# Absent rows read row 0 instead of needing cleared buffers, and Pool drains its finished transfers twice before the end

## The chip, the cores and the metric

The kernel runs on one core of a Trainium2 chip. The metric is the time of one execution on the device in microseconds (us), the median over several runs. Lower is better. A core has five engines that run side by side and wait for one another through semaphores: TensorE (PE, matrix products; PEld is its loading of weights), VectorE (DVE), ScalarE (ACT), GpSimd (Pool) and SyncE (SP, which here only issues transfers). Sixteen DMA engines move data between the main memory (DRAM) and the core's memory (SBUF). SP and ACT issue transfers through hardware queues. Pool issues its own through a software queue[...].

## What is computed

Two layers, one after the other.

```python
# attention with decay, in blocks of 64 positions: q, k, v are (4, 8, 768, 64)
intra = (qb @ kb.T * Dmask) @ vb
inter = (qb * lam_pow) @ kv_state
out[:, :, sl] = intra + inter
kv_state = lam_block * kv_state + (kb * rev_pow).T @ vb
...
# mixture of experts on the 3072 rows of 512 numbers that this gives
logits = xn @ en.T / tau          # x and the 8 expert embeddings, normalized
expert_idx = argmax(logits)       # one expert for each row
gate_w = softmax(logits)[expert_idx]
for e in range(8):
    h = maximum(x[mask] @ w1[e], 0)          # w1[e] is 512 x 1024
    out[mask] = gate_w[mask] * (h @ w2[e])   # w2[e] is 1024 x 512
```

Each row of the result belongs to one expert, so the second layer needs its rows sorted by expert.

## The kernel before

The work is ordered by hand (`tc.manual_schedule()`); every engine executes its instructions in the order in which the code writes them.

**The attention loop** (L774) runs over 24 tiles of 128 rows, `i` = 0 to 23. In each, PE transposes q and k (`pe_Tq`, `pe_Tk`), forms the scores (`pe_ST`, L383), multiplies them with v (`pe_O`) and updates the state (`pe_kv`). The finished tile is transposed back (`pe_X`) into `xg`, and `write_x` (L461) writes a group of tiles to the row store `x_dram`, one row of 272 words for each token: 512 numbers of 16 bits, then the gate's weight. A second set of steps routes the rows of a group as soon as it is complete: `pe_z`, `pe_sel`, `rt_a` to `rt_d`, `rt_n` (the norm, on Pool, L512) and `make_list`. These steps are hung on iterations by `at(i, slot, ...)`. The loop runs slot "pool" and then slot "w" at the end of an iteration. Groups have four tiles at first; the last two, 5 and 6 (GL), have two.

**The slots of the experts.** There are ten slots `r`. Experts 0 and 1 are split: slots 0 and 1 take their rows among the first 16 tiles, so that they can begin while attention still runs, and slots 2 and 3 take the rest. Slots 4 to 9 are experts 2 to 7. A slot has full tiles of 128 rows (2, 1 or 3 of them) and half a tile of 64 rows. The half tiles of two neighbouring slots share one tile, named `("h", r)`. That makes 24 full tiles and 5 shared ones, 29 in all, or 3712 places for 3072 rows. The rest stay empty.

**Row numbers.** The lists are built by matrix products of comparisons (`pe_list`) and added up in `lacc`. `decode` turns a list entry into a row number. An empty place comes out as LB = 4096, which is no row. `ids(r0, r1)` decodes the slots r0 to r1 - 1 into `lid` and puts the numbers of the shared tiles into `lh`.

**Gather and scatter.** `gather(r, g)` (L643) reads the 128 rows of tile g of slot r from `x_dram` into `x_e`. It is an indirect transfer with a bounds check: a place whose number is past the end is skipped, so its part of the buffer keeps what it held. For this reason `gather(r, None)` allocates the buffer and clears it with a Pool memset (L649) ahead of time: three buffers before the loop (L732), and twelve in the tail between attention and experts (L963 to L968). `put` (L900) multiplies a finished tile by the gate's weights on DVE and scatters the 128 rows to the output with an indirect transfer on Pool (L904), where empty places are skipped too. It then issues the gathers that the table `after` names for that place. There are 29 scatters; `n_scat[0]` counts them.

**Weights.** The weights of experts 0 to 2 are cast to 16 bits by their transfer, which the Pool queue issues: twelve transfers in the order expert 0 w1 (two halves), w2 (two halves), expert 1, expert 2. `load_w` issues the next one in slot "w" of the iterations 7, 9, 11, 13, 15, 16, 17, 18, 19, 20, 21 and 22. Those of experts 3 to 7 come later through SP in forty parts (`part_load`) and DVE casts them (`part_cast`).

**Early use.** Slots 0 and 1 are gathered in slot "pool" of iterations 19 (two tiles of slot 0), 20 (the shared tile and tile 0 of slot 1) and 21 (tile 1 of slot 1). PE transposes them in iterations 21, 22 and 23 (`early_xT`, L666).

**The tail and the experts** (from L961). The routing of the last group runs here: the norm on Pool (L512), `rt_c` on DVE (L562 is its first instruction) with the exponential on ACT (L568), the list, `ids(ES, NR)`, and the gathers of slots 2 and 3 and of their shared tile. Between these steps PE computes the first layer of slot 0 (`pe_L1`, L826, with ReLUs on ACT, L828). Then PE alternates first layers, second layers (`pe_L2`, L925, and `pe_L2h`, L934) and transposes of the next slot (`pe_xT`, `pe_xTh`) to the end.

**The close.** A branch (L1034) skips a part for slots that overflow. After it the program's last instructions (L1133) wait for all engines and drain them. Pool's queue has issued 12 weight loads, 29 gathers and 29 scatters by then.

Of the kernel before, what the change touches and what calls it, by code (L numbers as in the profile page):

```python
# [13 lines left out]
I32 = mybir.dt.int32  # L14
AF = mybir.ActivationFunctionType
ALU = mybir.AluOpType
# [4 lines left out]
def kernel(  # L21
# [12 lines left out]
    nc = tc.nc  # L34
    P = 128
# [19 lines left out]
    ES = 2  # L55
    TA = 16
    NR = ES + E
    HT = P // 2
    FULL = [2] * ES + [1] * ES + [3] * (E - ES)
# [4 lines left out]
    VR, GR = 32 * P, 4  # L64
    NL = NR * GR


    LB = 4096
# [15 lines left out]
    const = ctx.enter_context(tc.tile_pool(name="const", bufs=1))  # L84
# [12 lines left out]
    n_out = sum(FULL) + NR // 2  # L97
# [107 lines left out]
    lrow = const.tile([P, P], FP32, name="lrow")  # L205
    lacc = const.tile([P, NL], FP32, name="lacc")
    ltmp = const.tile([P, NL], FP32, name="ltmp")
    lid = const.tile([P, NL], I32, name="lid")
    lh = const.tile([P, NR // 2], I32, name="lh")
    nsq_all = const.tile([P, R], FP32, name="nsq_all")  # L210
    ohcum = [const.tile([P, E], FP16, name=f"ohcum{n}") for n in range(2)]
    en_n = const.tile([E, DC, 2, D], FP32, name="en_n")
# [233 lines left out]
    def pe_X(t):  # L446
        gi, j = group_of[t]
        if j == 0:
            xg[gi] = xgp.tile([P, 4, XW], I32, name="xg", tag="xg")
            nc.gpsimd.memset(xg[gi][:, :, DW:], 0)  # L450
        xv = xps.rearrange("p (u a d) -> p a u d", u=2, a=DC)
        for a in range(DC):
            nc.tensor.transpose(xv[:, a], xT_of(t, a), ident)  # L453
        sq = xtp.tile([P, DM], FP16, name="sq", tag="sq", bufs=1)
        nc.scalar.activation(sq, xps, AF.Square, accum_out=nsq_all[:, t : t + 1])  # L455
        nc.scalar.copy(xg[gi][:, j, 0:DW].bitcast(FP16), xps)
# [21 lines left out]
    def pe_sel(t):  # L478
        for s in range(2):
            gi, j = group_of[t - 1 + s]  # L480
            nc.tensor.matmul(z_of(gi)[:, j, :], zT[t][:, ds(P * s, P)], sel,
                             start=True, stop=True, skip_group_check=True)
# [25 lines left out]
    def rt_n(gi):  # L508
        tl = groups[gi]
        nt = len(tl)  # L510
        rt.setdefault(gi, {})["nrm"] = rsm.tile([P, 4], FP32, name="nrm", tag="nrm")[:, 0:nt]
        nc.gpsimd.tensor_tensor(rt[gi]["nrm"], nsq_all[:, tl[0] : tl[0] + nt], half[:, 0:nt],  # L512
                                op=ALU.pow)
# [94 lines left out]
    idl, xe, xTe, hT = {}, {}, {}, {}  # L608
    moe_x, moe_t = [moe_x1], [moe_t1]

    def decode(io, acc, tmp):
        nc.vector.scalar_tensor_tensor(tmp, acc, -1.0, acc, op0=ALU.mult, op1=ALU.min)
        nc.vector.scalar_tensor_tensor(tmp, acc, 0.0, tmp, op0=ALU.is_lt, op1=ALU.add)
        nc.vector.tensor_scalar(io, tmp, float(LB), None, op0=ALU.add)


    def ids(r0, r1):
        cols = slice(GR * r0, GR * r1)
        decode(lid[:, cols], lacc[:, cols], ltmp[:, cols])
        lr = lid.rearrange("p (n s g) -> p n s g", s=2, g=GR)  # L620
        r = r0
        while r < r1:
            q = r
            while q < r1 and FULL[q] == FULL[r]:
                q += 1
            nc.vector.tensor_copy(lh[0:64, r // 2 : q // 2], lr[0:64, r // 2 : q // 2, 0, FULL[r]])
            r = q
        nc.vector.tensor_copy(lh[64:128, r0 // 2 : r1 // 2], lr[64:128, r0 // 2 : r1 // 2, 1, 0])
        for r in range(r0, r1):
            g0 = r % 2  # L630
            idl[r] = lid[:, GR * r + g0 : GR * r + g0 + FULL[r]]
            if r % 2 == 0:
                idl["h", r] = lh[:, r // 2 : r // 2 + 1]


    def col0(r):
# [6 lines left out]
    def gather(r, g):  # L643
        if r not in xe:
            n = 1 if isinstance(r, tuple) else FULL[r]
            n1 = 1 if moe_x[-1] is moe_x1 else ES + NR // 2 - 1
            xe[r] = moe_x[-1].tile([P, n, XW], I32, name="x_e", tag=f"x_e{n}",
                                   bufs={1: n1, 2: ES, 3: E - ES}[n])
            nc.gpsimd.memset(xe[r], 0)  # L649
        if g is None:  # L650
            return
        first = r in range(ES) or r == ("h", 0)
        nc.gpsimd.indirect_dma_start(  # L653
            out=xe[r][:, g, :], out_offset=None, in_=x_dram[0 : TA * P] if first else x_dram[:],
            in_offset=bass.IndirectOffsetOnAxis(ap=idl[r][:, g : g + 1], axis=0),
            bounds_check=N - 1, oob_is_err=False)

    def xt_tile(r):
# [27 lines left out]
    def at(i, slot, fn, *a):  # L686
        todo.setdefault((i, slot), []).append((fn, a))
# [5 lines left out]
    for gi in range(GL):  # L693
        n = groups[gi][-1] + 1
# [14 lines left out]
        if n + 3 < R - 1:  # L709
            at(n + 3, "rank", lambda zr, gi=gi: pe_list(gi, zr[:, 64:128]))  # L710
            at(n + 3, "z", ev_list, gi)
            if gi == 3:
                at(n + 3, "z", ids, 0, ES)
    for i in (7, 9, 11, 13, 15, 16, 17, 18, 19, 20, 21, 22):
        at(i, "w", load_w, 1)
    for i, r, g in ((19, 0, 0), (19, 0, 1), (20, ("h", 0), 0), (20, 1, 0), (21, 1, 1)):
        at(i, "pool", gather, r, g)
# [11 lines left out]

    pool_ks(0)  # L730
    pool_ks(1)
    for r in (0, 1, ("h", 0)):  # L732
        gather(r, None)
    pe_Tk(0)
    pe_Tq(0)
    decay0(1)
# [105 lines left out]
    n_scat = [0]  # L842

    with (
# [15 lines left out]
        h = "h"  # L860
# [39 lines left out]
        def put(y_ps, r, g):  # L900
            y = moe_y.tile([P, DM], FP32, name="y_sb", tag="y_sb")
            nc.vector.tensor_scalar(y, y_ps, xe[r][:, g, DW : DW + 1].bitcast(FP32), None,  # L902
                                    op0=ALU.mult)
            nc.gpsimd.indirect_dma_start(  # L904
                out=out_views[n_scat[0]],
                out_offset=bass.IndirectOffsetOnAxis(ap=idl[r][:, g : g + 1], axis=0),
                in_=y[:],
                in_offset=None,
                bounds_check=N - 1,
                oob_is_err=False,  # L910
            )
            for x in after.get(n_scat[0], []):
                if x == h:
                    gather(pairs.pop(0), 0)
                else:
                    gather(*x)
            if n_scat[0] > 1:
                part_cast()
            n_scat[0] += 1

        def pe_L2(r, g):
            w = w_tiles[(expert(r), 2)]
            y_ps = ps_y.tile([P, DM], FP32, name="y_ps", tag="y")
            for fc in range(FC):
                nc.tensor.matmul(y_ps, hT[r][:, fc, ds(col0(r) + P * g, P)], w[:, fc, :],  # L925
                                 start=(fc == 0), stop=(fc == FC - 1))
            put(y_ps, r, g)
# [32 lines left out]

        pe_z(R - 1, kaz[:, 0:256])  # L961
        pe_X(R - 1)
        for x in (ES, ES + 1, ("h", ES)):  # L963
            gather(x, None)
        rt_n(GL)
        for r in range(2 * ES, NR, 2):
            for x in (r, r + 1, ("h", r)):
                gather(x, None)  # L968
        pe_sel(R - 1)
        rt_a(GL)  # L970
        rt_a2(GL)
# [10 lines left out]
        for gi in range(GL - 2, GL + 1):  # L982
            pe_list(gi, kaz[:, 320:384], first=(gi == GL - 2), last=(gi == GL))
        ev_list(GL)
        ids(ES, NR)
        gather(2, 0)
        gather(3, 0)
# [46 lines left out]
    with tc.If(mreg > 0, preferred_fallthrough_block=True, label="past"):  # L1034
        with (
# [11 lines left out]
            with tc.For_i(0, NR) as r:  # L1047
# [14 lines left out]
                with tc.For_i(0, end):  # L1062
                    l_ps = of_ps.tile([P, 1], FP32, name="of_l", tag="of_l")
                    for t in range(R):
# [12 lines left out]
                        in_offset=bass.IndirectOffsetOnAxis(ap=io[:, 0:1], axis=0),  # L1077
# [15 lines left out]
                    for fc in range(FC):  # L1093
# [44 lines left out]
```

## Time and profile before

| | before |
|---|---|
| time, median of 3 runs | 274.88 us (272.67 to 275.95) |
| span of the profiled execution | 266.9 us |
| PE busy | 240.6 us (90%) |
| DVE, ACT, Pool busy | 143.6, 123.0, 145.8 us |
| memsets of `x_e` (L649) | 15, from 314 to 768 ns each |
| Pool's transfers | 12 weight loads, 29 gathers, 29 scatters |
| gather on Pool (L653), scatter on Pool (L904) | medians 1,038 and 1,074 ns |
| weight load on Pool (L320, L322) | medians 788 and 783 ns |

Busy time is that of an engine's own instructions. Issuing a transfer from SP, waiting, branching and draining are not counted. The profiled execution is one run; its span ends with the last barrier. Two rates of PE's clock occur, 1.0 and 0.5 of full speed, and the profile gives their mean over a stretch as the granted clock. A transfer has two times, that of its issue by an engine and that of its landing, which the semaphore records give.

### The profile page before, as it was taken

To read this page: it belongs to the slowest core of one execution; us is meant where nothing else is said; L and a number is where in the kernel's file an instruction comes from. 1 tells how busy PE (TensorE), PEld (TensorE's weight loads), DVE (VectorE), ACT (ScalarE), POOL (GpSimd) and SP (SyncE) were. 2 spreads that over 40 slices of the span, in tenths; PEclk is the share of its full clock that TensorE was granted. 3 is DMA by queue.
4 is the path that set the end of the run, shared out by engine and by line. 5 is a ranking of instruction groups with operands and counts; after the bars stand their busy time and mean duration, and the time that the engine had idled before them with its cause. 6 is when DMAs were issued, how large, how long until landed. Compare 5 with 4: busy or idle time off the path is not lost. (4 is left out here: it accounts for less than half of the span.)

```text
span 266.9 us, 7432 instructions
## 1 busy us (share of the span) xinstructions
PE 240.6 (90%) x3011; PEld 168.1 (63%) x3012; DVE 143.6 (54%) x351; ACT 123.0 (46%) x277; POOL 145.8 (55%) x206
## 2 busy tenths in 40 slices
PE   7989999999999989986991999999999999999910
PEld 3777898897887887975871466745454545455400
DVE  1554576586576657762559556455626453551310
ACT  4754655654554544551461253746353545345100
POOL 7853536358238647419968087773838373722220
PEclk9999999999999999996898599999999999999985
DMA  7999999999999999947594599999899999943020
GB/s 154 237 221 218 211 207 214 273 232 226 209 228 206 232 240 232 187 114 146 99 152 133 153 360 372 307 398 377 272 337 268 417 323 305 290 156 119 22 92 0
DMA packets 79542, 59.64 MB, mean 223 GB/s; under 512 B 54660, under 2 KB 69000, under 8 KB 79506
## 3 DMA queue, kind: packets, MB, share of 16 engines
q1 hardware_dynamic: 71440, 42.51, 58.9%
q0 software_dynamic: 6976, 15.93, 24.8%
q10 hardware_dynamic: 1090, 0.70, 0.8%
q8 instruction: 24, 0.39, 0.6%
q14 instruction: 12, 0.10, 0.1%
HBM read 56.48 MB, written 10.94 MB: 253 GB/s over the span
## 5 line engine op out<-in xcount | busy, mean ns | idle before, releaser
L826 PE MATMUL h_ps<-xTe,w_sb 128*128 128x448 f16 (+2 forms) x312 | 52.9, 327 | 5.7 <-ACT hT L828 5.7
L828 ACT ACTIVATE hT<-h_ps 128x448 f16<-128x448 f32 (+2 forms) x78 | 37.0, 480 | 37.8 <-PE h_ps L826 36.0
L338 POOL TENSOR_TENSOR ks<-kn,kdec 128x512 f32<-128x512 f32 (+1 forms) x25 | 25.1, 1007 | 44.2 <-issue 21.7
L826 PEld LDWEIGHTS <-w_sb 128*128 128x128 f16 x320 | 30.7, 100 | 27.4 <-issue 6.2
L391 DVE TENSOR_TENSOR stm<-s_ps,step 128x512 f32<-128x512 f32 x48 | 30.9, 686 | 30.4 <-PE s_ps L383 30.4
L925 PE MATMUL y_ps<-w_sb,hT 128*128 128x512 f16 x192 | 45.0, 385 | 0.0
L902 DVE TENSOR_SCALAR y_sb<-y_ps,x_e 128x512 f32<-128x512 f32 x29 | 21.8, 751 | 41.5 <-PE y_ps L934 21.5
L904 POOL DMA_INDIRECT out_dram<-y_sb,lid x24 | 26.8, 1115 | 22.2 <-DVE y_sb L902 17.6
L653 POOL DMA_INDIRECT x_e<-x_dram,lid x24 | 26.2, 1090 | 19.1 <-DVE ohcum L553 7.1
L887 DVE CAST w_sb<-w_st 128x1024 f16<-128x1024 f32 x40 | 27.4, 706 | 12.4 <-DMA w_st<-in_moe_w_dram 12.3
L925 PEld LDWEIGHTS <-hT 128*128 128x128 f16 x192 | 18.3, 99 | 20.0 <-issue 1.7
L383 PE MATMUL s_ps<-qT,kT 64*64 64x128 f32 x768 | 27.8, 282 | 1.0 <-issue 0.7
L414 PE MATMUL o_ps<-stm,vn 128*64 128x128 f32 x384 | 27.1, 285 | 0.0
L383 PEld LDWEIGHTS s_ps<-qT,kT 64*64 64x64 f32 x768 | 21.6, 136 | 7.0 <-issue 5.4
L455 ACT ACTIVATE sq<-xps 128x512 f16<-128x512 f32 x24 | 14.3, 597 | 23.9 <-PE xps L453 22.6
L423 ACT COPY xT<-o_ps 128x256 f32<-128x256 f32 x24 | 8.9, 373 | 30.4 <-PE o_ps L414 30.4
L414 PEld LDWEIGHTS o_ps<-stm,vn 128*64 128x64 f32 x384 | 21.2, 140 | 2.6 <-issue 2.1
L359 DVE TENSOR_TENSOR qT<-q_ps,lamq 128x512 f32<-128x512 f32 x22 | 15.1, 686 | 3.8 <-PE q_ps L353 3.5
L585 POOL TENSOR_SCALAR l_row<-lrow,hl 128x128 f16<-128x128 f32 x22 | 13.2, 599 | 5.8 <-DVE hl L546 4.4
L369 PE MATMUL k_ps<-ident,ks 128*128 128x128 f32 x96 | 14.7, 274 | 0.7 <-POOL ks L338 0.7
L371 ACT COPY kT<-k_ps 128x512 f32<-128x512 f32 x24 | 14.3, 598 | 2.1 <-PE k_ps L369 2.1
L453 PE MATMUL xps<-ident,xT 128*128 128x128 f32 x96 | 15.1, 277 | 0.2 <-DVE xT L424 0.2
(148 smaller groups left out, 345.4 us busy)
## 6 DMA issues: line engine op xcount, KB each, us to landing
w_st<-in_moe_w_dram SPq DMA_DIRECT2D x40, 512.0 KB, 6.1
vn<-in_v_dram SPq DMA_DIRECT2D x24, 256.0 KB, 5.8
w_sb<-in_moe_w_dram POOLq DMA_DIRECT2D x12, 512.0 KB, 8.4
kn<-in_k_dram SPq DMA_DIRECT2D x23, 256.0 KB, 5.6
qn<-in_q_dram SPq DMA_DIRECT2D x11, 512.0 KB, 6.7
x_dram<-xg SPq DMA_DIRECT2D x8, 272.0 KB, 9.1
x_dram<-xg ACTq DMA_DIRECT2D x2, 272.0 KB, 8.0
x_dram<-xg SPq DMA_DIRECT2D x4, 136.0 KB, 5.6
```

The source lines that it names most:

```text
L338: nc.gpsimd.tensor_tensor(ks[i][:, h : h + n], kn[i][:, h : h + n], kdec[:, i % RB, h : h + n].unsqueeze(2).to_broadcast([P, n, D]), op=AL ...
L359: nc.vector.tensor_tensor(qT[j][:, :, :, s, :].rearrange("p a h i -> p h a i"), t.rearrange("p h (a i) -> p h a i", i=64), lamq[:, j % NC, ...
L383: nc.tensor.matmul(bank["s", h2][ds(64 * m, 64), hp, :], kT[i][ds(64 * h2, 64), hp, ds(64 * m, 64)], q_of(i, hp)[ds(64 * h2, 64)], start=( ...
L391: nc.vector.tensor_tensor(stm[i][:, h2], bank.pop(("s", h2)), step.unsqueeze(1).to_broadcast([P, HP, P]), op=ALU.mult)
L414: nc.tensor.matmul(bank["o", h2][ds(64 * u, 64), b2, :], vn[i][:, 2 * hp + h2, :], stm[i][:, h2, hp, :], start=(i % RB == 0 and b2 == 0), ...
L653: nc.gpsimd.indirect_dma_start(out=xe[r][:, g, :], out_offset=None, in_=x_dram[0 : TA * P] if first else x_dram[:], in_offset=bass.Indirec ...
L826: nc.tensor.matmul(h_ps[:, 0:n], w_chunk(w, c, fc), xTe[r][:, c, 0:n], start=(c == 0), stop=(c == DC - 1))
L828: nc.scalar.activation(hT[r][:, fc, 0:n], h_ps[:, 0:n], AF.Relu)
L887: nc.vector.tensor_copy(w[:, c, :] if which == 1 else w[:, 2 * c : 2 * c + 2, :].rearrange("p s d -> p (s d)"), staged.pop(0))
L902: nc.vector.tensor_scalar(y, y_ps, xe[r][:, g, DW : DW + 1].bitcast(FP32), None, op0=ALU.mult)
L904: nc.gpsimd.indirect_dma_start(out=out_views[n_scat[0]], out_offset=bass.IndirectOffsetOnAxis(ap=idl[r][:, g : g + 1], axis=0), in_=y[:], ...
L925: nc.tensor.matmul(y_ps, hT[r][:, fc, ds(col0(r) + P * g, P)], w[:, fc, :], start=(fc == 0), stop=(fc == FC - 1))
```

## The change

It has four parts.

- **No clearing.** `lid` and `lh` get a second copy of the row numbers. Copy 1 is as before and serves the scatters, so empty places are still not written. Copy 0 is taken modulo 4096 (one more DVE instruction in `ids`), so that an empty place reads row 0. It serves the gathers. Every place of a buffer is now written by its gather, with real numbers whose results nobody stores, and the memsets go: those before the loop, and those in the tail.
- **A drain in the tail.** Where the tail's memsets stood, Pool executes a drain. It is there to retire the transfers that have finished so far, which would otherwise be left for the drain of the program's close.
- **A drain six blocks from the close.** When all but six scatters have been issued, `put` has Pool drain again.
- **Later weight loads.** The iterations of `load_w` change from 16, 17, 18, 19, 20, 21, 22 to 19, 20, 20, 21, 21, 22, 22. This keeps loads out of iterations 16 to 18, in which k, v and a row-store write are still in transfer.

```diff
-    lid = const.tile([P, NL], I32, name="lid")
-    lh = const.tile([P, NR // 2], I32, name="lh")
+    lid = const.tile([P, 2, NL], I32, name="lid")
+    lh = const.tile([P, 2, NR // 2], I32, name="lh")
...
     def ids(r0, r1):
         cols = slice(GR * r0, GR * r1)
-        decode(lid[:, cols], lacc[:, cols], ltmp[:, cols])
+        decode(lid[:, 1, cols], lacc[:, cols], ltmp[:, cols])
+        nc.vector.tensor_scalar(lid[:, 0, cols], lid[:, 1, cols], LB - 1, None, op0=ALU.bitwise_and)
...
-            idl[r] = lid[:, GR * r + g0 : GR * r + g0 + FULL[r]]
+            idl[r] = lid[:, :, GR * r + g0 : GR * r + g0 + FULL[r]]
...
-            nc.gpsimd.memset(xe[r], 0)
-        if g is None:
-            return
...
-            in_offset=bass.IndirectOffsetOnAxis(ap=idl[r][:, g : g + 1], axis=0),
+            in_offset=bass.IndirectOffsetOnAxis(ap=idl[r][:, 0, g : g + 1], axis=0),
...
-    for i in (7, 9, 11, 13, 15, 16, 17, 18, 19, 20, 21, 22):
+    for i in (7, 9, 11, 13, 15, 19, 20, 20, 21, 21, 22, 22):
         at(i, "w", load_w, 1)
...
-    for r in (0, 1, ("h", 0)):
-        gather(r, None)
...
-                out_offset=bass.IndirectOffsetOnAxis(ap=idl[r][:, g : g + 1], axis=0),
+                out_offset=bass.IndirectOffsetOnAxis(ap=idl[r][:, 1, g : g + 1], axis=0),
...
             n_scat[0] += 1
+            if n_scat[0] == n_out - 6:
+                nc.gpsimd.drain()
...
         pe_X(R - 1)
-        for x in (ES, ES + 1, ("h", ES)):
-            gather(x, None)
         rt_n(GL)
-        for r in range(2 * ES, NR, 2):
-            for x in (r, r + 1, ("h", r)):
-                gather(x, None)
+        nc.gpsimd.drain()
         pe_sel(R - 1)
```

More of the change, by code (lines that the diff above doesn't have):

```diff
@@ L618, in ids @@
         cols = slice(GR * r0, GR * r1)
-        decode(lid[:, cols], lacc[:, cols], ltmp[:, cols])
-        lr = lid.rearrange("p (n s g) -> p n s g", s=2, g=GR)
+        decode(lid[:, 1, cols], lacc[:, cols], ltmp[:, cols])
+        nc.vector.tensor_scalar(lid[:, 0, cols], lid[:, 1, cols], LB - 1, None, op0=ALU.bitwise_and)
+        lr = lid.rearrange("p w (n s g) -> p w n s g", s=2, g=GR)
         r = r0
@@ L625, in ids @@
                 q += 1
-            nc.vector.tensor_copy(lh[0:64, r // 2 : q // 2], lr[0:64, r // 2 : q // 2, 0, FULL[r]])
+            nc.vector.tensor_copy(lh[0:64, :, r // 2 : q // 2], lr[0:64, :, r // 2 : q // 2, 0, FULL[r]])
             r = q
-        nc.vector.tensor_copy(lh[64:128, r0 // 2 : r1 // 2], lr[64:128, r0 // 2 : r1 // 2, 1, 0])
+        nc.vector.tensor_copy(lh[64:128, :, r0 // 2 : r1 // 2], lr[64:128, :, r0 // 2 : r1 // 2, 1, 0])
         for r in range(r0, r1):
             g0 = r % 2
-            idl[r] = lid[:, GR * r + g0 : GR * r + g0 + FULL[r]]
+            idl[r] = lid[:, :, GR * r + g0 : GR * r + g0 + FULL[r]]
             if r % 2 == 0:
-                idl["h", r] = lh[:, r // 2 : r // 2 + 1]
+                idl["h", r] = lh[:, :, r // 2 : r // 2 + 1]
     def col0(r):
```

## The prediction

> **What bounds the kernel now.** I read the page first: PE is busy 90% of the span, and the second section of it has three soft spots, PE at 6 tenths in slice 18, 1 in slice 21, and nothing in the last slices. So I asked for the busy time by stretch around them (columns: PE, PEld, DVE, ACT, POOL, granted clock, DMA share, GB/s).
>
> ```profile
> core 0: us, PE busy (x) PEld busy (x) DVE busy (x) ACT busy (x) POOL busy (x), PEclk, DMA share, GB/s
> ...
> 119.10:121.70 2.60, 0.02 (x2) 0.01 (x1) 1.15 (x7) 1.22 (x4) 2.29 (x3) 0.95 0.19 54
> 121.70:128.30 6.60, 5.97 (x78) 5.18 (x80) 1.33 (x3) 1.38 (x2) 6.11 (x10) 0.50 0.80 147
> ...
> 141.50:146.80 5.30, 0.00 (x0) 0.00 (x0) 5.13 (x7) 0.58 (x3) 4.25 (x8) 0.86 0.27 94
> 146.80:152.20 5.40, 5.38 (x25) 2.72 (x25) 3.14 (x19) 1.93 (x5) 0.00 (x0) 0.50 0.40 112
> 152.20:161.00 8.80, 8.80 (x61) 5.00 (x60) 4.09 (x6) 3.50 (x8) 6.65 (x6) 1.00 0.98 356
> 161.00:256.00 95.00, 93.09 (x596) 49.78 (x594) 44.90 (x69) 43.73 (x86) 52.25 (x54) 1.00 0.80 281
> ```
>
> Outside these holes PE is the bound. Hole A (119.1) and hole B (141.5) are each followed by a stretch at a granted clock of 0.50, so each costs more than its idle time. The timeline of all engines says what each waits for.
>
> ```profile
> 118.68 1.16 POOL L653 DMA_INDIRECT x_e<-x_dram,lid  x1 [5.47 <-DVE kv L441]
> ...
> 121.69 0.61 PE L666 MATMUL q_xtr<-ident,x_e 128*128 128x128 f16 x4 [2.58 <-DMA x_e<-x_dram,lid]
> ...
> 139.90 0.73 POOL L512 TENSOR_TENSOR nrm<-nsq_all,half 128x2 f32<-128x2 f32 x1 [1.01 <-ACT sq L455]
> ...
> 140.59 5.16 POOL L649 MEMSET x_e<- 128x816 int32 x9
> 140.66 5.12 DVE L562 TENSOR_SCALAR nrm<-nrm 128x2 f32<-128x2 f32 x1
> ...
> 146.22 0.21 ACT L568 ACTIVATE pe<-dz 128x16 f32<-128x16 f32 x1 [5.93 <-DVE dz L565]
> ...
> 146.82 3.36 PE L826 MATMUL h_ps<-xTe,w_sb 128*128 128x320 f16 x12 [5.32 <-ACT hT L828]
> ```
>
> Hole B: nine clearings run back to back on Pool, 140.59 to 145.75; a two-element DVE instruction of the router starts with them and ends with them. ACT sits behind it with the exponential, the ReLUs behind the exponential in ACT's order, and PE runs out of h_ps buffers. The view of that one DVE line shows how odd its 5.12 us is: the median of the seven is 183 ns.
>
> ```profile
> L562 DVE TENSOR_SCALAR nrm<-nrm x7: 152/183/5120, 41.8 to 140.7; 128x4 f32<-128x4 f32 x5, 128x2 f32<-128x2 f32 x2
> ```
>
> Hole A: PE waits for the first gather. The semaphore records show why Pool issues it only at 118.68: the x_dram write of group 3, issued by ACT at 109.06 and 109.78, lands at 117.0 and 117.8, 8.0 us later; the write of the last group, at 148.65 on idle DMA, needs 2.4. Between 105 and 118.6 the Pool queue's two weight loads take 47.8% of the 16 DMA engines' time (the DMA view of that window).
>
> The end: the last scatter is issued at 255.50 and lands at 258.0, but the span ends at 266.9. The views of the two closing lines (ns, least, median and most; first and last start):
>
> ```profile
> L1133 POOLq DRAIN x3: 46/103/5789, 260.0 to 266.6; - x3
> L1133 SPq DRAIN x3: 7/7/7, 260.6 to 266.0; - x3
> ```
>
> ```profile
> L1034 POOLq INC_SWDGE_SEM x1: 1600/1600/1600, 258.3 to 258.3; - x1
> ```
>
> One Pool DRAIN of 5,789 ns at 260.0, 2 us after everything has landed, and all engines wait for it at the last barrier (265.8). Pool's other three drains in the trace, with no transfer of the program newly behind them, take 184, 103 and 46 ns.
>
> **What the Trainium skill says.** "SBUF — State Buffer", section "SBUF: two separate sides": DVE and GpSimd share a port pair under an exclusive lock, and the second comer fully blocks. The trace agrees (183 ns becomes 5,120 beside the clearings), and shows the wait lasting over all nine. "TensorE: Matmul & The Clock Gate", Part 1: an idle array falls back to half clock and needs some 3.4 us of work to return. The trace agrees in kind: 0.50 after both holes, for 6.8 and 6.9 us. "VectorE: DVE Perf Modes", section "The DRAIN you can't avoid": boilerplate drains cost about 12 ns on all engines. SP's 7 agrees, Pool's 5,789 does not. No page prices that drain.
>
> **The change part by part.**
>
> (1) The final drain. Pool has issued 12 weight loads, 29 gathers and 29 scatters: 70 transfers. I read 5,789 as 0.1 us plus a price for each finished transfer not yet retired: 5.69/70 = 81 ns. Two earlier drains leave six scatters: 0.1 + 6 x 0.081 = 0.6 us. Saving **5.2** on the path that sets the end. Bounds: 0 if the 5.8 is fixed; 6.8 if the 1.6 of INC_SWDGE_SEM falls too.
>
> (2) The drain six blocks from the close follows scatter 23, issued at 238.63 here. It has 24 gathers and 23 scatters to retire, 47 x 81 ns = 3.8 us, and must see scatter 23 land (3.2 us after issue here). Behind it on Pool stand scatters 24 and 25 (240.58, 242.31), then nothing until 250.21. Even at 5.8 us it ends at 245.9, both scatters at 248.5. The y_sb pool has six buffers and DVE frees PSUM without Pool, so nobody waits: 0.
>
> (3) The twelve late clearings, 5.16 + 0.85 us, go. The nine hold hole B. Without them L562 takes 0.2 and PE waits about 0.4 (the ReLU follows the exponential), so 4.9 of 5.3 us idle go; 146.8 to 152.2 then runs at full clock, 5.4 -> 2.7. Sum 7.6. The three early ones (1.31 us at 8.30) are hidden: Pool afterwards waits for kn until 12.58 anyway. Beside them DVE gets one more instruction in ids, by the row of its neighbour L614 0.18 us, about 0.2 with its wait, before the first late gather.
>
> (4) The tail drain stands behind rt_n on Pool. Queued behind it are the gathers of slots 2 and 3, for which PE's transposes wait. It has 17 transfers to retire (1.4 us), but an unfinished one I take it to wait for, so what counts is when the last weight load lands. Loads 6 to 12 now go out at iterations 19, 20, 20, 21, 21, 22, 22. Seven at some 3 us each on the queue (5.7 to 9.2 us from issue to landing, several overlapping) reach from about 117 to 144 or 145. The gather of slot 2, at 152.83 now, would be due near 144 with hole B closed and the shift of (5); it is then 1 us late, and PE has little slack (it landed at 159.5, used at 160.94). Cost **1.0**; bounds 0 and 4.
>
> (5) Loads 6 to 8 leave iterations 16 to 18, so k and v finish earlier and the group-3 write lands in about 3 us instead of 8.0, by 113. The first gathers then go at 113.5 and 114.9, land before 119, and hole A vanishes: 3.2 us idle (2.58 + 0.63) plus about 2.3 of the half-clock stretch: from L383 start to L383 start iterations 20 and 21 last 9.49 and 6.72 us, elsewhere 4.6 to 5.0 (104.37, 108.99, 113.98), and the gathered transposes need 1.0; 16.2 - 9.6 - 1.0 is about 5.5. Gain 5.5. But the gather of (1, 1) now stands behind two loads of iteration 20 on Pool (0.8 us each) and on the queue: issued near 129.2, landing near 132, while PE would want it at 129.3. That gives back about 3.0 with the clock. Net **2.5**; bounds 0 and 5.5.
>
> (6) Row 0 for absent rows. Slots hold 29 x 128 = 3712 rows for 3072 tokens: 640 extra reads of 1088 B. Page section 3 gives the Pool queue 6976 packets for 24.8% of 16 x 266.9 us, 152 ns a packet; four rows to a packet (4,352 B in the records), 160 packets / 16 engines x 152 ns = 1.5 us of DMA in a stretch where DMA is 0.80 busy and PE bound. I take 0.5 on the path. Bounds: 0, and rival 3.
>
> Sum: -5.2 - 7.6 + 0.2 + 1.0 - 2.5 + 0.5 = -13.6 us; 274.88 - 13.6 = **261.3**.
>
> **Rivals.** 1, the wait is only replaced: Pool's drain holds DVE as the clearings did, or waits much longer for the loads, and the late (1, 1) gather eats hole A. Left is the end, 5.2, and perhaps 2: 267.7. For it: Pool is busy without a break from 118.68 to 138 already, and gets more loads there. Against: a drain writes no tile. 2, both holes vanish whole: -5.2 - 7.6 - 5.5 = 256.6. For it: weight loads alone on DMA took about 3 us or less each. 3, slower: reads of one row serve one after another at a whole packet time, 152 ns. By the reference's routing of these inputs most half-tile gathers hold 48 to 64 absent rows; 64 x 0.152 = 9.7 us. Their slack between landing and use is 2.9, 1.4, 2.6, 7.6 and 1.8 us, so PE loses about 6.8 + 8.3 + 7.1 + 2.1 + 7.9 = 32, less 13.6: 293. Against: 0.7 MB in all is little; but no transfer of this trace reads one row many times, so nothing here prices it. 4, same: the 5.8 us drain is fixed and the tail drain gives hole B back: 272 to 275.
>
> **How the numbers follow.** Forecast 0.57, rival 1 0.17, rival 2 0.13, rival 3 0.06, rival 4 0.07. Range 255.5 to 268.5: it takes in rivals 1 and 2 with the bound of INC_SWDGE_SEM, leaves out 3 and 4. Faster by over 1%: 0.87; within: 0.06; slower: 0.07.
>
> **What would show it.** The last Pool DRAIN under 1 us; L562 under 0.3 us everywhere; granted clock 1.0 near 147; no wait for x_e at L666 in iteration 21, perhaps a new one in 23; a Pool DRAIN at the tail ending with the last w_sb landing; PE from the slot-2 transposes to the last L925 still 93 to 95 us. I am wrong if the final DRAIN stays near 5.8, if DVE is held beside the tail drain, or if PE now waits at L666 for half-tile gathers.

## The result, and the profile after

The changed kernel takes **263.89 us** (median of four runs, 261.91 to 265.63) against 275.35 us before (four runs; the table ahead of the prediction has the first three): a ratio of 0.960, with a 95% interval of 0.951 to 0.969. A second measurement, in a later batch of runs, gave 263.56 against 274.61 us, ratio 0.963 (0.957 to 0.969). The forecast was 261.3 us.

One thing must be said before the traces are laid side by side. The first trace of before is of an execution of 268.6 us, while its times lie at 272.7 to 276.0. The experiments below suggest why: on one chip the kernel before takes 267.3 us, and its traces lack a slow stretch that the traces from the other chips show. So the traces of two kernels are compared here step by step, never by their spans alone. The intervals leave out runs more than 1.5% above the fastest of the same kernel; for one kernel below that leaves two of twelve, and five of seventeen in its repeat, so medians of all runs stand beside the ratios.

**The close.** The drains and the semaphore instruction of the changed kernel, one source line each (ns, least, median and most; first and last start in us):

```profile
L1129 POOLq DRAIN  x3: 46/103/538, 262.4 to 263.6; - x3
...
L1030 POOLq INC_SWDGE_SEM  x1: 320/320/320, 262.0 to 262.0; - x1
...
L919 POOLq DRAIN  x1: 5307/5307/5307, 241.6 to 241.6; - x1
...
L964 POOLq DRAIN  x1: 6795/6795/6795, 138.6 to 138.6; - x1
```

The last drain falls from 5,789 to 538 ns, and the semaphore instruction at the branch from 1,600 to 320. From the issue of the last scatter to the end of the span it is now 263.9 - 258.7 = 5.2 us, where it was 266.9 - 255.5 = 11.4. The two new drains (L964 in the tail, L919 six blocks from the close) take 6.8 and 5.3 us, at places where Pool has time.

**The middle.** The timeline of the changed kernel (start, length, engine, line, instruction; in brackets the idle time before it and what ended it; DMA_INDIRECT at L653 is a gather, a transfer that takes its rows from a list of row numbers; line numbers are one or two off those of the kernel before in places):

```profile
114.10 1.18 POOL L653 DMA_INDIRECT x_e<-x_dram,lid  x1 [1.79 <-DMA x_dram<-xg]
...
119.51 0.61 PE L666 MATMUL q_xtr<-ident,x_e 128*128 128x128 f16 x8
...
131.84 0.58 PE L666 MATMUL q_xtr<-ident,x_e 128*128 128x128 f16 x4 [1.93 <-DMA x_e<-x_dram,lid]
...
139.36 0.17 DVE L563 TENSOR_SCALAR nrm<-nrm 128x2 f32<-128x2 f32 x1
...
140.56 1.79 PE L824 MATMUL h_ps<-xTe,w_sb 128*128 128x320 f16 x12 [0.37 <-ACT hT L826]
...
148.01 1.30 POOL L653 DMA_INDIRECT x_e<-x_dram,lid  x1 [8.69 <-PE h_ps L824]
...
153.03 0.40 PE L666 MATMUL xtr<-ident,x_e 128*128 128x128 f16 x4 [0.82 <-DMA x_e<-x_dram,lid]
...
158.36 0.40 PE L666 MATMUL xtr_h<-ident,x_e 128*128 128x128 f16 x4 [3.21 <-DMA x_e<-x_dram,lh]
```

Read it from the top. Hole A is gone: the first gather goes at 114.1 instead of 118.7, and PE transposes at 119.51 without a wait. A smaller hole, C, has come at 131.84, for the late gather of (1, 1). Hole B is gone: the DVE instruction takes 0.17 us instead of 5.12, and PE waits 0.37 us. Then comes a hole that before did not have: PE waits 0.82 and 3.21 us for the gathers of slot 2. I call it D.

Busy time by stretch of the changed kernel (us and number of PE, PEld, DVE, ACT, Pool; granted clock; DMA share; GB/s):

```profile
core 0: us, PE busy (x) PEld busy (x) DVE busy (x) ACT busy (x) POOL busy (x), PEclk, DMA share, GB/s
117.00:122.00 5.00, 4.51 (x89) 3.99 (x89) 3.76 (x16) 2.94 (x6) 4.49 (x6) 1.00 0.89 161
...
131.80:139.00 7.20, 7.16 (x67) 5.04 (x68) 1.45 (x9) 3.99 (x9) 2.93 (x7) 0.76 1.10 221
139.00:143.00 4.00, 3.57 (x33) 2.23 (x32) 3.29 (x20) 2.51 (x7) 0.33 (x1) 1.00 1.10 236
143.00:153.00 10.00, 9.20 (x62) 5.13 (x60) 5.25 (x15) 3.50 (x8) 4.07 (x4) 1.00 0.94 309
153.00:158.40 5.40, 2.17 (x13) 0.97 (x14) 2.55 (x4) 0.59 (x1) 4.18 (x5) 1.00 1.01 297
158.40:176.30 17.90, 13.63 (x97) 9.14 (x98) 4.51 (x7) 6.42 (x19) 10.17 (x10) 0.81 0.73 269
176.30:257.60 81.30, 81.30 (x488) 41.04 (x485) 36.93 (x58) 36.57 (x67) 38.46 (x41) 1.00 0.77 262
```

The clock is 1.00 where hole B's after-effect was, and 0.76 over the stretch behind hole C (half clock for 3.4 us of it). The last row is as long as before: from the last transposes of slot 4 to the last product, 81.0 us in both traces. So all that the middle gained or lost is settled by 176. DMA is full from 131.8 to 158 (the printed share can pass 1.00), in the stretch where it stood at 0.27 and 0.40 beside hole B. And 158 to 176 is only three quarters busy.

Four marks show where the time went, from the traces of before and after: PE's first second-layer product, the issue of slot 2's first gather, its transposes, and the last transposes of slot 4.

| us from the start | before | after | moved |
|---|---|---|---|
| first product of L925 | 150.3 | 142.4 | -7.9 |
| first gather of slot 2 issued | 152.8 | 148.0 | -4.8 |
| first transposes of slot 2 | 160.9 | 153.0 | -7.9 |
| last transposes of slot 4 | 173.0 | 176.3 | +3.2 |
| last scatter issued to the end | 11.4 | 5.2 | -6.2 |

A gain of 7.9 us at 142 is gone by 176, if these two traces may be compared. Two theories follow. **A**: the parts add up as predicted, and the loss in 158 to 176 belongs to something else than the change. **B**: the change refilled the hole itself, by the tail drain or the bunched loads, and only the close is won.

### The profile page after: what moved, and what is told of

It reads as the page before. It is cut to its first block, busy times and chain, and to the rows that moved or that the text cites. A ratio compares the mean times of both kernels' runs of the same rounds, so it can differ in the third digit from the quotient of the medians.

```text
span 263.9 us, 7404 instructions
## 1 busy us (share of the span) xinstructions
PE 241.5 (91%) x3011; PEld 167.5 (63%) x3012; DVE 138.9 (53%) x353; ACT 123.3 (47%) x277; POOL 137.6 (52%) x191
## 3 DMA queue, kind: packets, MB, share of 16 engines
q0 software_dynamic: 6976, 16.63, 25.9%
## 5 line engine op out<-in xcount | busy, mean ns | idle before, releaser
L925 PE MATMUL y_ps<-w_sb,hT 128*128 128x512 f16 x192 | 46.7, 395 | 0.0
L902 POOL DMA_INDIRECT out_dram<-y_sb,lid x24 | 26.2, 1090 | 31.8 <-DVE y_sb L900 22.2
L653 POOL DMA_INDIRECT x_e<-x_dram,lid x24 | 26.3, 1096 | 17.1 <-PE h_ps L824 8.7
L925 PEld LDWEIGHTS <-hT 128*128 128x128 f16 x192 | 18.6, 101 | 20.6 <-issue 2.1
L384 PE MATMUL s_ps<-qT,kT 64*64 64x128 f32 x768 | 26.9, 275 | 0.3 <-DVE qT L356 0.3
L384 PEld LDWEIGHTS s_ps<-qT,kT 64*64 64x64 f32 x768 | 20.9, 132 | 6.2 <-issue 4.5
L674 ACT COPY xTe<-xtr 128x512 f16<-128x512 f16 (+1 forms) x14 | 10.8, 770 | 10.1 <-PE xtr L666 7.4
```

Source lines behind the costliest of these rows:

```text
L384: nc.tensor.matmul(bank["s", h2][ds(64 * m, 64), hp, :], kT[i][ds(64 * h2, 64), hp, ds(64 * m, 64)], q_of(i, hp)[ds(64 * h2, 64)], start=( ...
L653: nc.gpsimd.indirect_dma_start(out=xe[r][:, g, :], out_offset=None, in_=x_dram[0 : TA * P] if first else x_dram[:], in_offset=bass.Indirec ...
L902: nc.gpsimd.indirect_dma_start(out=out_views[n_scat[0]], out_offset=bass.IndirectOffsetOnAxis(ap=idl[r][:, 1, g : g + 1], axis=0), in_=y[: ...
```

## The experiments

Each ratio is against the kernel before, run beside it on the same chip, with its 95% interval; the last column is the median of all runs against that of before. The chips are numbered in the order of the experiments; each batch of runs had one chip, so a difference between chips may also be one between batches. On which chip the first measurements of before and after were made isn't on record.

| run | chip | ratio | medians, us |
|---|---|---|---|
| both drains alone | 1 | 0.986 (0.979 to 0.993) | 271.31 / 276.5 |
| row 0 alone | 1 | 0.978 (0.969 to 0.986) | 274.59 / 276.5 |
| moved loads alone | 1 | 0.987 (0.980 to 0.994) | 273.09 / 276.5 |
| changed, old loads | 1 | 0.967 (0.959 to 0.975) | 269.0 / 276.5 |
| before again | 2 | 1.003 (1.000 to 1.006) | 268.03 / 267.28 |
| changed, no tail drain | 2 | 0.964 (0.958 to 0.970) | 257.43 / 267.28 |
| changed, two weight stages | 2 | 1.052 (1.045 to 1.059) | 281.16 / 267.28 |
| changed, gathers spread | 2 | 0.978 (0.971 to 0.984) | 260.45 / 267.28 |
| changed again | 3 | 0.963 (0.957 to 0.969) | 263.56 / 274.61 |
| row 0 alone again | 3 | 0.984 (0.978 to 0.989) | 271.51 / 274.61 |
| changed, one load at 16 | 3 | 0.962 (0.954 to 0.969) | 265.10 / 274.61 |
| changed, loads at 16 and 17 | 3 | 0.958 (0.954 to 0.962) | 262.61 / 274.61 |

### The drains alone

```diff
 (kernel before, with its memsets and its loads)
+            if n_scat[0] == n_out - 6:
+                nc.gpsimd.drain()
...
+        nc.gpsimd.drain()
         pe_sel(R - 1)
```

> The kernel before with the two drains of the change alone; clearings and weight loads stay as they were. Theory A (the parts add up as predicted, with the close as the traces show it): the last Pool DRAIN falls from 5,789 to about 540 ns and INC_SWDGE_SEM from 1,600 to 320, so 5.2 to 6.5 us less; the tail drain finds its loads landed by then (the old loads end earlier) and costs nothing: 269 to 270 against 275.35. Theory B (only the close gains, and the tail drain costs a few us at the gathers of slot 2): 271 to 273. A third: each drain costs what it takes off the last one, 275.

Measured: 271.3 us, 5.2 under before by the medians, and 3.8 by the ratio (1.4% of 276.5). The last drain takes 534 ns and the semaphore instruction 320. The DVE instruction of hole B still takes 5,120 ns here. So the size doesn't decide: 5.2 is the low end of theory A (5.2 to 6.5 us less), and 3.8 lies in theory B (2.4 to 4.4). The trace speaks for A: the first gather of slot 2 leaves at 150.57, 3.3 us after the last x_dram write is issued, where the kernel before took 3.5, so the tail drain costs nothing there.

### Row 0 alone, twice

```diff
 (changed kernel)
-    for i in (7, 9, 11, 13, 15, 19, 20, 20, 21, 21, 22, 22):
+    for i in (7, 9, 11, 13, 15, 16, 17, 18, 19, 20, 21, 22):
...
-            if n_scat[0] == n_out - 6:
-                nc.gpsimd.drain()
...
-        nc.gpsimd.drain()
```

> The kernel before with absent rows reading row 0 and no clearings; no drains, weight loads as before. Theory A: the vector instruction at L562 takes under 0.3 us, hole B is gone and the stretch after it runs at full clock: 7 us less, about 268; the last DRAIN stays near 5.8 us. Theory B (the gain of the middle is lost again where the gathers of slot 2 wait for the last x_dram write, and in the sparse stretch of PE after them): hole B is gone all the same, but the slot-2 gathers come no earlier in step, and no more than 2 us are left at the end: 273 to 275.

> The same kernel as before in the row-0-alone run (no clearings, row 0 read for absent rows, no drains, old loads), now to be set beside the changed kernel on one chip. Theory A with S: on a chip without the stretch the whole gain of hole B stays, 6 to 7 us under before (ratio 0.974 to 0.978); on one with it, 2 to 5 us (ratio 0.98 to 0.993). Theory B (what hole B gave is lost at the slot-2 gathers everywhere): ratio 0.99 or more on both.

Measured: 1.9 and 3.1 us under before by the medians, 6.2 and 4.5 by the ratios. Hole B is gone in both traces; the line's own view, in the second:

```profile
L563 DVE TENSOR_SCALAR nrm<-nrm x7: 152/171/221, 41.8 to 140.1; 128x4 f32<-128x4 f32 x5, 128x2 f32<-128x2 f32 x2
```

The seventh, at 140.1, has no 5.12 us any more, and PE's first product of L925 comes at 143.1 to 143.3. But the last transposes of slot 4 come at 175.8 and 178.7, 22 to 24 us after the first of slot 2, where the first trace of before had 12.1. So removing the hole works as theory A says, and less than the 7 us of A is left at the end. No drain and no moved load is in this kernel, so the cause that B names in the section on the result (the tail drain or the bunched loads) is wrong. How much is really lost depends on what before needs for this stretch, and a second trace of it, below, asks that.

### The loads alone, and the changed kernel without them

```diff
 (kernel before)
-    for i in (7, 9, 11, 13, 15, 16, 17, 18, 19, 20, 21, 22):
+    for i in (7, 9, 11, 13, 15, 19, 20, 20, 21, 21, 22, 22):
```

> The kernel before with the moved weight loads alone. Theory A: the group-3 x_dram write lands near 112 to 113 instead of 117 to 118, hole A (2.6 us, and half clock behind it) goes and a shorter one comes at the gather of (1, 1): 2.5 us less, about 273. Theory B: the loads bunched into iterations 19 to 22 lie in front of the last gathers and the x_dram write, and give it back: 275 to 277.

> The changed kernel with the weight loads at their old iterations. Theory A: hole A comes back, the late gather of (1, 1) goes: 2.5 us slower than the changed kernel, 266.4. Theory B: with the last weight load landing earlier the tail drain ends at once and the last x_dram write lands in some 2.5 us instead of 4.5, so the gathers of slot 2 come earlier and the sparse stretch of PE at 158 to 172 goes: equal or faster than the changed kernel, 261 to 264.

Measured: the loads alone give 3.4 to 3.6 us. In their trace the first gather goes at 113.6 and PE transposes at 119.2 without a wait. In the changed kernel with the old loads hole A is back: PE waits 3.25 us for the transposes of slot 0, till 122.5. Its ratio is 0.967 against 0.960 and 0.963 with the new ones, in other batches and with overlapping intervals, so what the loads are worth inside the whole change isn't resolved. Theory B of this run is out: the tail drain takes 2.25 us and ends at 144.0, yet the first gather of slot 2 leaves only at 150.59, and PE waits 0.65 and 2.92 us in hole D.

The parts multiply: drains 0.981, row 0 0.993 and 0.989, loads 0.988 (medians, from two chips) give 0.958 to 0.962 together, and the medians of the changed kernel give 0.958 and 0.960. By the ratios of the table the product is 0.952 and 0.957, against 0.960 and 0.963. So no part is seen to spoil another, as far as these intervals reach.

### Before again: the stretch goes with the chip or the batch

> The kernel before, unchanged, for a second trace of it: the first one was of an execution of 268.6 us, 6 to 7 us under the median of its times. Theory S (a stretch between the transposes of slot 2 and those of slot 4, in which VectorE and ScalarE see TensorE's results some us late, is in most executions of every kernel here, and the first trace of before happened to lack it): 275 us, and the stretch from the first transposes of slot 2 to the last of slot 4 takes 18 to 25 us instead of the 12.1 of the first trace. Theory B (the stretch is what the change did): 12 us there again, and the 6 us come from elsewhere, as from the clock in the first 120 us.

Measured: neither, as stated. On this chip the kernel before takes 267.28 us (265.0 to 269.2 in 23 runs of it, 268.03 in the 20 of the copy), and its stretch from slot 2 to slot 4 is 12.1 us again. The changed kernels traced on this chip need 14.5 and 14.9 us for it, which is hole D, and 18.8 in the one whose casts wait for their loads. All eight traces from chips 1 and 3, and the first one of after, have 20 to 25 us. Two of the eight, drains alone and loads alone, still have the clearings of before. The first trace of before is like chip 2's. From 275.35 us, less 1.7 outside the span and 93.9 from the last slot-4 transposes to the end, those transposes come at some 179.8 in the runs of before that were timed: an estimate, since none of those was traced. The trace of after is of its slowest run (265.63 us); from its median of 263.89 the same sum, with 87.6 us to the end, gives 174.6. So the table's +3.2 turns into a gain of some 5 us, and this with the 6.2 of the close makes up the 11.5 us between the medians.

What the stretch looks like, in the timeline of this run and then in that of after:

```profile
162.23 2.80 PE L826 MATMUL h_ps<-xTe,w_sb 128*128 128x192 f16 x32
...
162.76 2.64 ACT L828 ACTIVATE hT<-h_ps 128x192 f16<-128x192 f32 x8 [1.41 <-PE h_ps L826]
```

```profile
161.39 2.42 PE L824 MATMUL h_ps<-xTe,w_sb 128*128 128x192 f16 x20
...
162.85 0.33 ACT L826 ACTIVATE hT<-h_ps 128x192 f16<-128x192 f32 x1 [0.26 <-issue]
...
164.75 0.33 ACT L826 ACTIVATE hT<-h_ps 128x192 f16<-128x192 f32 x1 [1.57 <-issue]
165.14 0.49 PE L824 MATMUL h_ps<-xTe,w_sb 128*128 128x192 f16 x4 [1.33 <-issue]
166.90 0.33 ACT L826 ACTIVATE hT<-h_ps 128x192 f16<-128x192 f32 x1 [1.81 <-PE h_ps L824]
167.28 0.49 PE L824 MATMUL h_ps<-xTe,w_sb 128*128 128x192 f16 x4 [1.65 <-ACT hT L826]
168.33 0.33 ACT L826 ACTIVATE hT<-h_ps 128x192 f16<-128x192 f32 x1 [1.10 <-PE h_ps L824]
```

Eight ReLUs follow one another in 2.64 us above. Below, five groups of products are complete by 163.8, and the ReLUs of the third, fourth and fifth start at 164.75, 166.90 and 168.33, that is 0.9, 3.1 and 4.5 us later, though ScalarE executes nothing in between. PE then waits for the ReLUs, having three `h_ps` buffers. Why is open.

One more thing sets these traces apart. The first trace of before and the four from chip 2 hold 4,397 to 4,409 records of semaphores each; the nine with the stretch hold 3,657 to 3,837, and no view of them gives a landing time. Instructions are not lost: 7,404 are recorded of the changed kernel, and as many of the one with spread gathers from chip 2. So what the brackets name as a releaser in those nine rests on incomplete records, and the recording of the trace itself, on chips or in batches where records are lost, is a possible cause of the stretch that no run tested.

### The tail drain

```diff
 (changed kernel)
-        nc.gpsimd.drain()
         pe_sel(R - 1)
```

> The changed kernel without the drain in the tail; the one before the close stays and has then some 64 transfers to retire, 5.3 us at 82 ns, still hidden. Theory A (the last x_dram write, landing at 147.2, is what the gathers of slot 2 wait for, and the drain ends before it): 264 within 1 us, final DRAIN about 0.6 us. Rival (the drain holds Pool and with it the gathers): 260 to 262.

Measured: ratio 0.964, as with the drain (0.960 and 0.963, in other batches). The drain before the close and the last one, of this run:

```profile
L919 POOLq DRAIN  x1: 6600/6600/6600, 235.4 to 235.4; - x1
...
L1128 POOLq DRAIN  x3: 46/103/548, 256.4 to 257.7; - x3
```

The close drain has 17 transfers more to retire and takes 1,293 ns more than in the changed kernel (5,307), 76 ns for each. It is hidden at this length too: 81.0 us from the last transposes of slot 4 to the last product, as with the drain. And hole D is there without a tail drain:

```profile
150.33 1.32 POOL L653 DMA_INDIRECT x_e<-x_dram,lid  x1 [9.25 <-PE h_ps L824]
...
155.52 0.40 PE L666 MATMUL xtr<-ident,x_e 128*128 128x128 f16 x4 [1.56 <-DMA x_e<-x_dram,lid]
...
159.86 0.40 PE L666 MATMUL xtr_h<-ident,x_e 128*128 128x128 f16 x4 [2.22 <-DMA x_e<-x_dram,lh]
```

The gather goes at 150.33, 5.5 us after the last x_dram write is issued (144.8); with the drain, 5.0 us after it (143.0). So the drain isn't what holds it. In the changed kernel it ends at 145.4, when the last weight load has landed (144.6). The tail drain neither costs nor, with the close drain there, gains anything measurable.

The same gap tells over all fourteen traces what hole D goes with. From the last x_dram write's issue to the first gather of slot 2 it is 3.3 to 3.6 us in the four traces of kernels that clear (moved loads or tail drain among them), and 4.5 to 6.8 us in the ten that read row 0, with old loads or new ones, with the tail drain or without.

### Two tries at the stretch

```diff
 (changed kernel: two weight stages)
-        tc.tile_pool(name="wst", bufs=4) as wst,
+        tc.tile_pool(name="wst", bufs=2) as wst,
...
-        for _ in range(4):
+        for _ in range(2):
             part_load()
 (changed kernel, another run: gathers spread)
-        after = {1: [(4, 0), (4, 1)], 2: [(4, 2), h], 3: [(5, 0), (5, 1)], 4: [(5, 2)], 5: [(6, 0)],
...
+        after = {1: [(4, 0), (4, 1)], 2: [(4, 2)], 3: [h], 4: [(5, 0)], 5: [(5, 1)], 6: [(5, 2)],
...
```

> The changed kernel with two staging buffers for the experts' weights instead of four, so two loads of 512 KB under way instead of four. If the late stretch after slot 2 comes from the weight stream filling the DMA engines (0.98 to 1.00 busy there): the stretch shrinks from 23 towards 12 us, 254 to 258, unless the casts now wait for their loads, which would show as DVE waits for w_st in the later slots and 265 or more. If it comes from elsewhere: 23 us as before, 264 to 266.

> The changed kernel with the gathers of slots 4 to 9 spread, one behind each scatter where two stood, so that Pool's indirect transfers do not follow each other without a break at 151 to 168. If the late stretch comes from Pool's chain of indirect transfers: the stretch shrinks from 23 us to 12 to 16, 254 to 260. If not: 264 within 2 us, or a us or two more where a gather now comes late.

Both ran on chip 2, where there is no stretch to remove, so they say nothing on its cause. What they do say: two stages are too few. The waits of the first one's DVE and PE, from 170 to 280 (us in all, times, longest):

```profile
DVE w_sb L885 <- DMA w_st<-in_moe_w_dram: 49.6, 27, 4.3
```

```profile
PE y_ps L925 <- DVE y_sb L900: 16.5, 4, 6.6
```

DVE stands 49.6 us before its casts (11.6 in the kernel with four stages and no tail drain), and PE waits behind it for `y_ps`, the buffers of its results: 23.7 us slower than that kernel on the same chip. It also says something on hole D: with two `w_st` loads on their way instead of four, the gather leaves no sooner after the write (4.9 us), but the shared tile needs 5.5 us from issue to use where the other run on this chip with the tail drain needs 7.1, and PE waits 2.0 us there instead of 3.5. Spreading the gathers is 3.0 us slower than the kernel without the tail drain, and from the last transposes of slot 4 to the last product PE takes 84.1 instead of 81.0 us, with waits at L666 for the shared tiles.

Up to the third scatter the kernel with spread gathers equals the changed one, so it also gives the pair before and after on one chip. The first product of L925 moves from 148.0 to 142.4 (-5.6), the gather of slot 2 from 150.6 to 147.8 (-2.8), the last transposes of slot 4 from 170.4 to 168.0 (-2.4). PE waits 0.83 and 2.63 us in hole D, and not at all there in before. Without the stretch, too, less than half of the middle's gain arrives in this pair.

On this chip the traces show no gain from the moved loads. The last group of products ahead of hole B (the place of hole B, in the changed kernels) starts at 138.5 in before, at 139.6 with spread gathers and at 141.3 without the tail drain. Hole A cost before less here than in its first trace (1.82 and 0.81 us of waiting, half clock for 3.4 us instead of 6.8), and hole C cost more (3.07 and 3.15 us of waiting, half clock for 3.4 and 6.8).

### Closing hole C

```diff
 (changed kernel: one load at 16; another run: loads at 16 and 17)
-    for i in (7, 9, 11, 13, 15, 19, 20, 20, 21, 21, 22, 22):
+    for i in (7, 9, 11, 13, 15, 16, 19, 20, 21, 21, 22, 22):
+    for i in (7, 9, 11, 13, 15, 16, 17, 19, 20, 21, 21, 22):
```

> The changed kernel, unchanged, beside the others of this batch. Theory S (the late stretch belongs to some of the chips): on a chip that has it, about 264 against 275 and a stretch of about 23 us between the first transposes of slot 2 and the last of slot 4; on a chip without it, about 256 against 267 and a stretch of 14 to 15 us. Ratio 0.955 to 0.965 either way.

> The changed kernel with one of the two weight loads of iteration 20 put into iteration 16, long before the group-3 x_dram write. If the gather of (1, 1) is late because of the loads ahead of it on Pool's queue: it is issued one load earlier, hole C (the wait at L666 in iteration 23, 1.9 to 3.2 us and half clock after it) shrinks to under 0.5 us, hole A stays closed, and with the last weight load landing some 3 us earlier the gathers of slot 2 are no later than now: 3 to 5 us faster than the changed kernel. Rival: the load at 16 delays k and v in the full DMA stretch before 100, and the write of group 3 with them: no faster, or slower.

> As the run with one load moved to iteration 16, and a second one moved to 17. If loads before iteration 18 are done by the time group 3 is written (109): 1 to 2 us faster than with one moved, by an earlier last load and x_dram write. If the load of iteration 17 reaches into 109 to 113: the group-3 write lands late, hole A comes back in part, and it is slower than with one moved.

The changed kernel again: 263.56 us, on a chip with the stretch, as theory S says, and 20.4 us of it. One load at 16, timeline:

```profile
130.51 0.40 PE L666 MATMUL q_xtr<-ident,x_e 128*128 128x128 f16 x4 [0.30 <-DMA x_e<-x_dram,lid]
...
139.54 3.61 PE L925 MATMUL y_ps<-w_sb,hT 128*128 128x512 f16 x16
...
147.01 1.33 POOL L653 DMA_INDIRECT x_e<-x_dram,lid  x1 [10.54 <-PE h_ps L824]
...
151.61 0.61 PE L666 MATMUL xtr<-ident,x_e 128*128 128x128 f16 x4 [2.26 <-DMA x_e<-x_dram,lid]
```

Hole C falls from 1.93 to 0.30 us, no half clock follows, and PE reaches L925 at 139.5, 2.6 us sooner than in the changed kernel on this chip (142.1). The mechanism was as expected; the gain was not: 265.10 and 262.61 us stand on both sides of 263.56, with overlapping intervals. The gather of slot 2 leaves at 147.0, only 0.8 us sooner, 6.8 us after the last x_dram write was issued at 140.2. Full DMA is the reason that the traces offer: from 130 to 142 its share is 1.05 here. With a second load at 17, hole A comes back in part (0.81 us of waiting) and the wait for (1, 1) is 0.64; the gather of slot 2 leaves at 145.9, and PE still waits 2.42 us for it. That the time is the lower of the two lies within the intervals. No version tried beats the changed kernel by more than the intervals.

## Why the prediction was right, and where its terms were off

The total (261.3) lies 2.3 to 2.6 us under the measured 263.9 and 263.6, inside the range. Part of that is luck: the close gave 1.0 us more than forecast and the middle some 3 less, 5.2 instead of 8.4 (7.6 + 2.5 - 0.2 - 1.0 - 0.5), taken to the medians as above. Step by step:

1. **The final drain: right, and low in the trace.** 538 ns against 0.6 forecast; the price of a transfer is (5,789 - 538)/64 = 82 ns against 81. The semaphore instruction, held as a bound, falls too, by 1.3 us. So 6.2 us are saved between the last scatter and the end, where 5.2 were forecast. The two drains alone gave 3.8 to 5.2.
2. **The close drain hidden: right.** 5.3 us, and 6.6 us without the tail drain; PE's 81.0 us are untouched.
3. **Hole B: right where it lies, too large at the end.** DVE 0.17 us, PE's wait 0.37, full clock. From the group of products before the hole (140.79, and 139.49 after) to the end of the first sixteen products of L925 (154.81, and 146.01) PE needs 7.5 us less, against 7.6 forecast; on chip 2 it is 7.1. As a part by itself row 0 brought 1.9 to 6.2 us instead of about 7. What failed is the "Sum 7.6" taken as time on the path to the end.
4. **The tail: inside its bounds, wrong cause, and the mis-sized term.** The prediction took 1.0 us for the late gather of slot 2, from bounds of 0 and 4, and laid it to the tail drain and the last weight load. PE loses 0.82 + 3.21 = 4.0 us there, 3.5 to 3.8 us on chip 2, with the tail drain or without. The gather leaves 5.0 us after the last x_dram write is issued where it was 3.5 before (4.8 with row 0 alone), and the shared tile then needs 7.1 us from issue to use. DMA idled around the write in before and is full around it now; that this delays the write is inferred. It isn't the moved weight loads, since the gap is as long with the old ones; the first `w_st` parts lengthen the shared tile's gather, as the run with two stages shows, and not the gap. Here is the mis-sized term: 1.0 predicted, 3.5 to 4.0 shown. It outweighs the 1.0 us that the close gave beyond its forecast and makes most of the miss.
5. **The moved loads: right in what happens, the size open.** Hole A vanished, the new wait for (1, 1) came in iteration 23 with half clock behind it; 3.4 to 3.6 us alone against 2.5 on chip 1, 1.3 us at the group before hole B in the first pair of traces, and a loss of 1.0 and 2.7 us there on chip 2. How long the half clock lasts after either hole (3.4 or 6.8 us) is part of these differences.
6. **Row 0: no serial reads.** 64 reads of one row at 152 ns each would have held a shared tile 9.7 us. The traces of changed kernels on chip 2 give landings too: 4.0 us after the issue for the first shared tile, 6.5 and 7.0 for slot 2's, against 3.8 and 5.8 in the first trace of before, and at most 8.0 for any gather, against 8.3 in before on that chip. Rival 3 is out. The packets of Pool's queue stay at 6,976, since an absent row had its place in a packet before too; the bytes rise by 0.70 MB, and the queue's share times the span from 66.2 to 68.4 us, 2.2 us of DMA against the 1.5 forecast.

One sign that the prediction named for being wrong did come: PE waits at L666 for a half-tile gather, 3.21 us. It was meant for serial reads, which step 6 excludes; here it marks the late write and gather of step 4. Another sign failed as well: from the transposes of slot 2 to the last product PE needs 104.6 us in the trace of after, not 93 to 95, and 95.9 in the run without the tail drain, where there is no stretch.

Of the rivals, the first is right in part: a wait did take the place of the one removed. But it is a DMA wait at slot 2, and not Pool's drain holding DVE: L563 takes its 0.17 us at 139.36 while the tail drain runs (138.6 to 145.4). The stretch after it was foreseen by no step; by the times it lies in before as in after, and so cancels in part. How much of row 0's gain it takes, against hole D, isn't settled, nor is its cause.

## What to carry to other kernels

A hole that is closed is worth what arrives at the next place where an engine waits for data. Follow the gain to that place and ask whether the transfer there moves forward by as much; when DMA was idle during the hole, as here, it may be the one that is late. A cost at the very end, such as the drain of unretired transfers, has nothing behind it that could swallow the gain, and can be moved under work that hides it. And when a trace and the times of the same kernel disagree by some per cent, take a second trace beside the times before explaining anything.

## What the runs showed of the hardware

- A Pool drain costs about 82 ns for each of Pool's transfers not yet retired (an estimate from 5,789 ns for 70 and 538 for 6), and INC_SWDGE_SEM at the branch about 20 ns each (from 1,600 and 320). Earlier drains take this over, at 76 ns each in the one place where the number was varied.
- Gathers in which many places read one and the same row aren't read one by one: shared tiles land 4.0 to 7.0 us after their issue, 3.8 and 5.8 with those places skipped, where 64 reads at 152 ns each would need 9.7.
- One and the same kernel takes 267.3 us on one chip and 274.6 to 276.5 on two others. The traces of its variants from those two have a stretch of 20 to 25 us where its own on the first has 12 us; chip, batch and the recording of the trace are not told apart.
- PE's clock stays at a half after a hole in pieces of 3.4 us: stretches of 3.4, 6.8 and 10.2 us occur, and the same hole is followed by 3.4 us in one trace and 6.8 in another (hole A of before: 6.8 and 3.4). A wait of 1.93 us was enough to bring it (hole C), one of 0.37 us wasn't (the rest of hole B). The Trainium skill, "TensorE: Matmul & The Clock Gate", Part 1, gives some 3.4 us of work to return to full clock; the shortest of these pieces agrees, and the longer ones are multiples of it.
